# New orders for the first of two attention blocks, 46 instead of 42 projections in pairs, and four new figures in the planner

## Chip, core and metric

The kernel runs on one core of one Trainium2 chip. The metric is the device time in microseconds (us); a time stands for several runs by their median. The core has five engines that each work through their own list of instructions: TensorE (PE in the profile; its weight loads are PEld), VectorE (DVE), ScalarE (ACT), GpSimd (POOL) and SyncE (SP), which here issues all the DMAs. They wait for each other by semaphores only.

## What is computed

Two independent attention layers, A and B, each on 2048 tokens of width 512 with 32 heads of 16. Their outputs stand side by side.

```python
qkv = (x @ wqkv).reshape(B, S, 3, H, Dh).transpose(2, 0, 3, 1, 4)
q, k, v = qkv[0], qkv[1], qkv[2]
scores = einsum("bhqd,bhkd->bhqk", q, k) * (Dh ** -0.5)
# A only: idx = arange(S); d = idx[:, None] - idx[None, :]
# A only: scores = where((d >= 0) & (d < 256), scores, -1e9)
o = einsum("bhqk,bhkd->bhqd", softmax(scores), v)
y = o.transpose(0, 2, 1, 3).reshape(B, S, D) @ wo
out = concatenate([y_A, y_B], axis=-1)
```

## The kernel before

**Blocks and units.** Layer A is the first block, layer B the second. A unit is a block, a group g of four heads (0 to 7) and a chunk c of 512 queries (0 to 3): 32 units for each block. A's window lets one query tile see at most three key tiles, so A has little attention work for each unit; B sees all 16.

**Projections.** Queries and keys are projected for a pair of groups p (0 to 3) and a chunk c, values for a chunk c and a token tile a: 32 + 32 + 32 = 96 projections over both layers, all of them made during the first block. Each is 12 matmuls of 512 columns (four slices of the contraction times three products of split float32 parts). `ORDER_P` names them in their order: `Ak12` is layer A, keys, p = 1, c = 2; `Bv30` is layer B, values, chunk 3, tile 0. A projection runs either alone over all 128 rows (`project_qk`, `project_v`, by `products`, L212), or in a pair over two halves of 64 rows (`half_rows`, L340): 24 steps of two concurrent matmuls into two banks, cut into four parts.

Its result leaves PSUM over ACT. For queries and keys (`end_qk`) it is then split into two parts, by POOL (L305, L306) or, for the first group, by ACT and DVE (L291, L301), stored in device memory (`parts`), and read back by `load_k` and `load_q` in the layout that scores need (`opk`, `oq`). Values go to `vd` and come back into `vt`.

**Attention in block A.** For each unit, `max_item` makes score products and their row maxima (L505 on PE, L510 or L514 and L515 on DVE). `max_finish` turns them into three bf16 parts (L567). `max_rows` transposes these on PE (L582), and ACT (`ntr`) and two small DMAs write them as extra rows of `oq` (L589). `scores` (L615) then gives scores less the maximum, ACT takes the exponential (L622), POOL cuts the window's edge (L632), and `weigh` (L661) multiplies by the values. `unit_end`, `invert` and `normalise` bring sums and outputs through device memory.

**The order.** `ORDER_A` writes out PE's order in the first block, one letter for each item:

- `p` a projection alone (PE's full array), `g` one of the four parts of a pair
- `m` a maximum item for two heads, `e` the same for B's first unit from separate copies
- `s` scores of two heads for one step, `w` the weighing of one step (three steps to a unit)
- `t` the transpose of a unit's maxima

p uses the full array, g, m, e and s use row tiles, w and t column tiles. The loop over `todo_a` takes one letter after the other. The order of everything else follows from the class `Model`, a small clock with costs for each engine: `M.run` adds a duration to an engine, `M.dma` an issue on SP, a transfer and a landing, with eight lanes in flight. Follow-up steps wait in the heap `soon` (`after`), loads in `lists`, and both are put into the program as soon as the modelled PE time has reached the modelled time of their operands. The model places instructions only; on the chip each of them waits for its real operands, and each engine keeps its list's order.

PSUM has seven banks for all of this (`M.banks["u"]`) and one for the weighed sums. An m takes two neighbouring banks, an s two, a p one, and a pair two from its first part to its last.

**Block B** runs by fixed patterns (`ORDER`, `LAST`) that neither string touches; the model's figures are used there too, for the place of transfers.

Of the kernel before, what the change touches and what calls it, by code (L numbers as in the profile page):

```python
# [48 lines left out]
FILL = 16  # L49
WARM = 22  # L50
ORDER_P = (
# [4 lines left out]
    "Bk23 Bq21 Bk31 Bk33 Bq22 Bq30 Bq31 Bq10 Bq33 Bk32 Bq32 Bk30 ").split()  # L56
WAKE = 200
LOAD = 105
LEAD = 1400
# [2 lines left out]


ORDER_A = (
    "pppppppmmppmmpmmggmmpptmgmgmmppmmggmmpmsgmsgmmpmstwsmgmmgswssgmsgmmwtgmsgmmpmsgmsgmmpsmwtmswsmswsmmp"
    "smswsmmwtsswmsgsgsmwsmgmgmgmgswmsgmgmtwmsgmsgmswmgmsgmmpsmmwtsmwmspsmwsmmpssmwmstwmmspsmswsmmpmmwsmm"
    "swtsmspmmwsmpmsstwmsmwmsssmwmmmpmsmpmtsmwsmmswmmswssmpsmtwsmswmsmsmmmwmspsmwssmtmwmmswmgmsgmswsmgmmg"
    "mwtsmsmmmmpsmwsssmmwtmswmsmpsmmsmwsmwmsmtsmmswmsmpmmswtmsmswsmsmwssmpmmmwtpsmswmmgmgsmsgmwtmsgsmwmmm"
    "psmswwssspmmspmmtwpmsgmsgmmwwsgmsgmgmsgsmtwwmsgsmgmgsmgswsmgmswsmgmwsmgmsgmstwmsgmsgmwmmstwwssmpsmsw"
    "smgmsgmmpsmgmgmmwtmswmsmpmsmwsmsmmswtmsmpmswsmswmmswtsmsmwmsmpsmswtmmmpmsmwsmwmgsgmstwmsgmsgsewmmmpm"  # L70
    "mgsgmswsmgesgeswmmgmgetwsegsmgmswemspmmswmswesgesgmstwsmgmmgmpemmpesmwtwemmpmsgsmgsmwsgsmgemwmstwmmm"
    "pmsgmsgeswsegesgmswmsgmsgeswsmgsmgmwmsmpmmmpmmspmmmtwww")
LAND = 700
LAND_V = 0
LGAP = 2500
# [4 lines left out]
class Model:  # L80
# [19 lines left out]
        return self.run("PE", turn + ns, *after)  # L100

    def dma(self, kb, *after):
        t = self.run("SP", 450, *after, self.lanes[0]) + 600
        self.t["DMA"] = max(self.t["DMA"], t) + int(4.0 * kb)

        self.lanes = [*self.lanes[1:], self.t["DMA"] + 1300]
        return self.lanes[-1]

    def bank(self, pool, n=0):
# [33 lines left out]
def attention_kernel(ctx: ExitStack, tc: tile.TileContext, xT, wqk, wv, wo, out):  # L143
# [9 lines left out]
    M = Model()  # L153
# [131 lines left out]
    def end_qk(b, p, s, c, bank, ps):  # L285

        n = f"{b}_{p}_{s}_{c}"
        at_most(project_qk, 1)
        two = sb.tile([128, 2, QC], F32R, name=f"st_{n}", tag="st")
        if (b, p) == (0, 0):  # L290
            op = nc.scalar.activation(two[:, 0], ps, AF.Copy)  # L291
            t1 = mark(op, M.run("ACT", 480, M.t["PE"] + WAKE))
        else:
            raw = row(f"raw_{n}")
            op = nc.scalar.activation(raw, ps, AF.Copy)  # L295
            t1 = mark(op, M.run("ACT", 480, M.t["PE"] + WAKE))
            release(bank, t1)

        def sub():
            if (b, p) == (0, 0):  # L300
                nc.vector.tensor_sub(two[:, 1], ps, two[:, 0].bitcast(F32))  # L301
                t = M.run("DVE", 610, t1)
                release(bank, t)
            else:
                nc.gpsimd.tensor_copy(two[:, 0], raw)  # L305
                nc.gpsimd.tensor_sub(two[:, 1], raw, two[:, 0].bitcast(F32))  # L306
                t = M.run("Pool", 2400, t1)
            after(t, lambda: store(t), (project_qk, b, p, s, c))

        def store(t):  # L310
            if (b, p, s) not in parts:
                parts[b, p, s] = dram.tile([2, 128, S], F32, name=f"parts_{b}_{p}_{s}")
            nc.sync.dma_start(parts[b, p, s][:, :, c * QC:(c + 1) * QC].rearrange("p r t -> r p t"), two.bitcast(F32))
            ready["parts", b, p, s, c] = M.dma(512, t)
            slots_st.pop(0)
            slots_st.append(ready["parts", b, p, s, c])
        after(t1, sub, (project_qk, b, p, s, c))

    since = []

    def mark(op, t):

        since.append((t + M.load, len(since), op))
        return t
# [341 lines left out]
    def row(n, shape=(128, QC)):  # L666
        return sb.tile(list(shape), F32, name=n, tag="row", bufs=5)
# [122 lines left out]
    def after(ns, f, key=None):  # L790
        seq[0] += 1
        heapq.heappush(soon, (ns, seq[0], f, key))
# [6 lines left out]
    def at_most(kind, n):  # L799

        while sum(x[3] is not None and x[3][0] == kind for x in soon) > n:
            heapq.heappop(soon)[2]()
# [16 lines left out]
    def bank(n=0):  # L819
        return M.bank("u", n)  # L820
# [9 lines left out]
    def release(b, t):  # L830
        if b is not None:
            M.release(b, t)
# [26 lines left out]
    def operands(it, n=0):  # L859

        f, b, *a = it
        if f == project_qk:
            keys = [("w", b, a[0], a[1])] + [("x", b, a[2], i) for i in range(4)]
            t = (slots_st + [M.NEVER] * 2)[n] - 2700 + LAND_V
        elif f == project_v:
            keys = [("w", b, "v", i) for i in range(4)] + [("x", b, a[0], i) for i in range(4)]
            t = (slots_v + [M.NEVER] * 2)[n] - 2700 + LAND_V
        else:
            keys = [("w", b, "o", i) for i in range(4)] + [("o", b, i, a[0]) for i in range(4 if len(a[1]) == 1 else 3)]
            t = 0  # L870
        return max(t, *(ready.get(k, M.NEVER) for k in keys))
# [133 lines left out]
    while todo_a or gen[0]:  # L1005
# [13 lines left out]
        t = NEVER  # L1019
        if gen[0]:  # L1020
            t = pe
        elif x == "p":
            t = max(bank(), operands(its_a[nb]))
        elif x == "g" and stage == 0:
            t = max(bank(1), operands(its_a[nb]), operands(its_a[nb + 1], int(its_a[nb][0] == its_a[nb + 1][0])))
        elif x == "g":
            t = min(since)[0] if CHUNK * stage == 12 else pe
        elif x == "t" and nts:
            t = max(ready["nm", *nts[0]] + LOAD, bank())
        elif x == "w" and k < i:  # L1030
            un, (m, pieces), a, z = flat[k]
            t = max(*(ready.get(("v", 0, un[1] // 2, y[0]), NEVER) for y in pieces), ready["p", *un, m] + 100,
                    M.bank("o") if a else 0)
        elif x == "s" and i < k + AHEAD and (max_rows, *flat[i][0]) in made:
            t = max(bank(1), ready["q", *flat[i][0]] + LAND)
        elif x == "e":
            t = max(ready.get(("qe",), NEVER), ready.get(("ke", early[ne][2]), NEVER)) + LAND + 1500
            t = max(t, M.pair(), M.t["DVE"] - 300)
        elif x == "m" and not (mxs[nm][2] and (nts or mxs[nm][0][0] and ne < len(early))):
            un, it, z = mxs[nm]  # L1040
            t = max(*(ready.get(("k", *un[:2], c), NEVER) for c in (range(NQC) if un[0] else range(un[2] + 1))),
                    ready.get(("qd", *un), NEVER)) + LAND
            t = max(t, M.pair())
# [105 lines left out]
    while nq < 4 * len(steps):  # L1149
# [3 lines left out]
        for x in ORDER if nm < len(mx) else LAST:  # L1153
            k = ns // HG
            if x == "s" and k < len(steps):
                if ns % HG == 0:
                    t = k * STEP
# [28 lines left out]
            elif x.isdigit():  # L1186
# [19 lines left out]
                elif int(x) == 4 and nm < len(mx):  # L1206

                    t = k * STEP
# [37 lines left out]
```

## Time and profile before

| | |
|---|---|
| median of 3 runs | 1816.94 us (1816.69, 1816.94, 1822.71) |
| profiled execution | 1815.08 us, span 1813.4 us |
| mean granted TensorE clock | 0.998 |
| busy: PE, DVE, ACT, POOL | 99%, 83%, 77%, 36% of the span |
| block A | 0 to about 529 us |
| block B | about 529 us to the end |

In the tables of stretches each engine has its busy time in us and, in brackets, its instructions; then come the granted clock of TensorE (1.00 is full speed), the mean busy share of the 16 DMA engines and what they moved. In lists by time each row has the start and the length in us, the engine, the line and what was written and read; in square brackets stands how long the engine had been idle, and who ended that. PE's ends are modelled, so starts are the better measure. A row with a line first gives a group: its count, its busy time, the mean ns of one, and the idle time ahead of it.

### The profile page before, as it was taken

How to read it: one execution, taken by the hardware profiler on the slowest of the kernel's cores; microseconds unless marked ns; L12 is line 12 of the kernel's file. 1: busy time of each engine (PE TensorE's matmuls, PEld its weight loads, DVE VectorE, ACT ScalarE, POOL GpSimd, SP SyncE). 2: the span in 40 equal slices, each digit the busy share in tenths (PEclk: the TensorE clock that was granted, in tenths of full speed). 3: DMA queues.
4: the chain of work that ended last, by engine and by line, in shares of the span. 5: the costliest groups of instructions: out<-in, count | busy, mean ns of one | idle time of the engine just before them, and what ended most of it. 6: DMA issues, size and time to landing. Idle time of an engine off the chain costs nothing. (4 is left out here: it accounts for less than half of the span.)

```text
span 1813.4 us, 39043 instructions
## 1 busy us (share of the span) xinstructions
PE 1795.6 (99%) x14982; PEld 912.2 (50%) x14982; DVE 1508.8 (83%) x2243; ACT 1398.4 (77%) x2750; POOL 649.0 (36%) x1334
## 2 busy tenths in 40 slices
PE   9999999999999999999999999999999999999998
PEld 6776566767764455444444444444444444443436
DVE  5556776676779776899999999999999999999901
ACT  4465666655569776799999999999999999999983
POOL 0377778664755431042310024320112422022330
PEclk9999999999999999999999999999999999999999
DMA  7766667544573222311201211130031121010012
GB/s 248 218 189 208 190 195 231 173 154 140 162 213 102 77 85 67 82 29 49 61 20 31 63 42 29 29 78 16 16 76 35 29 64 37 17 54 16 24 37 93
DMA packets 129162, 166.80 MB, mean 92 GB/s; under 512 B 23012, under 2 KB 58852, under 8 KB 128964
## 3 DMA queue, kind: packets, MB, share of 16 engines
q1 hardware_dynamic: 128976, 164.31, 30.8%
q8 instruction: 118, 1.93, 0.4%
q14 instruction: 68, 0.56, 0.1%
HBM read 94.49 MB, written 68.19 MB: 90 GB/s over the span
## 5 line engine op out<-in xcount | busy, mean ns | idle before, releaser
L622 ACT ACTIVATE p<-ps_all 128x512 f32<-128x512 f32 x2432 | 1258.1, 597 | 185.0 <-PE ps_all L615 118.6
L462 DVE TENSOR_REDUCE mt<-ps_all 128x2 f32<-128x1024 f32 x1516 | 1195.0, 870 | 63.5 <-PE ps_all L458 52.0
L615 PE MATMUL ps_all<-oq,opk 51*128 51x512 f32 (+2 forms) x2752 | 775.2, 405 | 3.8 <-ACT p L622 2.6
L458 PE MATMUL ps_all<-opk,oq 48*128 48x512 f32 x2016 | 674.5, 438 | 0.4 <-DVE mt L462 0.2
L646 PE MATMUL ps_all<-p,vt 128*17 128x256 f32 (+1 forms) x6056 | 587.7, 460 | 0.5 <-ACT ou L672 0.5
L615 PEld LDWEIGHTS ps_all<-oq,opk 51*128 51x128 f32 x2752 | 398.9, 185 | 181.8 <-ACT p L622 157.7
L458 PEld LDWEIGHTS ps_all<-opk,oq 48*128 48x128 f32 x2016 | 308.7, 184 | 316.5 <-DVE mt L462 179.2
L632 POOL TENSOR_SCALAR_AFFINE_SELECT p<-p 128x256 f32<-128x256 f32 x480 | 178.5, 407 | 111.6 <-ACT p L622 105.1
L646 PEld LDWEIGHTS ps_all<-p,vt 128*17 128x17 f32 x6056 | 100.7, 95 | 223.3 <-issue 212.7
L532 POOL TENSOR_TENSOR mu<-mt 128x16 f32<-128x16 f32 x31 | 6.8, 220 | 508.5 <-DVE mt L462 508.5
L514 DVE COPY_PREDICATED ps_all<-mone,ps_all 128x256 f32<-128x256 uint16 x224 | 95.3, 425 | 99.0 <-PE ps_all L505 89.8
L515 DVE TENSOR_REDUCE nm<-ps_all 128x2 f32<-128x512 f32 x224 | 155.2, 693 | 7.7
L700 POOL TENSOR_TENSOR rd<-ld,minus 128x32 f32<-128x32 f32 x15 | 81.9, 5458 | 218.6 <-DMA ld<-od 218.6
L340 PE MATMUL ps_all<-x,w 64*128 64x512 f32 x672 | 119.9, 392 | 0.0
L212 PE MATMUL ps_all<-x,w 128*128 128x512 f32 x432 | 109.2, 401 | 1.3 <-DVE x L162 0.7
L505 PE MATMUL ps_all<-opk,oq 48*128 48x384 f32 (+2 forms) x512 | 95.7, 369 | 3.8 <-ACT p L622 1.5
L661 PE MATMUL ps_all<-p,vt 128*17 128x384 f32 (+2 forms) x1408 | 97.5, 392 | 0.3 <-POOL p L632 0.2
L212 PE MATMUL ps_all<-w_o,x_o 128*128 128x512 f32 x384 | 92.7, 396 | 0.6 <-ACT ob L765 0.6
L212 PEld LDWEIGHTS ps_all<-x,w 128*128 128x128 f32 x432 | 78.8, 189 | 24.7 <-issue 3.3
L340 PEld LDWEIGHTS ps_all<-x,w 64*128 64x128 f32 x672 | 86.1, 185 | 7.9 <-ACT raw L295 0.3
L295 ACT ACTIVATE raw<-ps_all 128x512 f32<-128x512 f32 x56 | 32.5, 597 | 73.3 <-PE ps_all L212 56.7
L212 PEld LDWEIGHTS ps_all<-w_o,x_o 128*128 128x128 f32 x384 | 70.6, 188 | 30.3 <-issue 12.8
(77 smaller groups left out, 954.1 us busy)
## 6 DMA issues: line engine op xcount, KB each, us to landing
parts<-st SPq DMA_DIRECT2D x64, 512.0 KB
oq<-parts SPq DMA_DIRECT2D x128, 128.0 KB
opk<-parts SPq DMA_DIRECT2D x128, 128.0 KB
od<-ou SPq DMA_DIRECT2D x64, 256.0 KB
vd<-vst SPq DMA_DIRECT2D x32, 272.0 KB
oq<-parts SPq DMA_DIRECT2D x128, 64.0 KB
opk<-parts SPq DMA_DIRECT2D x128, 64.0 KB
t<-od SPq DMA_DIRECT2D x32, 256.0 KB
```

Of the source, the lines that this page charges most:

```text
L212: nc.tensor.matmul(ps, l(u), r(v), start=start and k == 0, stop=stop and k == n - 1)
L340: op = nc.tensor.matmul(view(banks[a ^ turn]), l(u)[rows], r(v)[rows], start=turn == q == 0, stop=turn == 1 and q == 11)
L458: nc.tensor.matmul(ps[:, n], q[rows, 128 * qt:128 * qt + 128], k[rows, kc * QC:kc * QC + QC], start=True, stop=True)
L462: op = nc.vector.tensor_reduce(out=m[:, a:a + len(heads), r, qt, kc], in_=ps, axis=AX.X, op=ALU.max)
L505: nc.tensor.matmul(two[:, a, 0:w], opq[b, g, c][rows, r, 128 * qt:128 * qt + 128], opk2(g)[rows, r, t0:t1], start=True, stop=True)
L514: nc.vector.copy_predicated(two[:, :, 256:384], later, two[:, :, 0:128])
L515: op = nc.vector.tensor_reduce(out=m[:, :, r, qt, 0], in_=two[:, :, 128:384], axis=AX.X, op=ALU.max)
L615: nc.tensor.matmul(ps[x][:, col:col + n1], opk2(g)[rows, pr, 128 * k:128 * k + 128], opq[b, g, c][rows, pr, q0:q0 + n1], start=True, stop= ...
L622: op = nc.scalar.activation(p[:, a0 + x, :w], ps[x][:, :w], AF.Exp, scale=SCALE)
L632: nc.gpsimd.affine_select(out=v, in_=v, pattern=[[0, 2], [sign, 128]], compare_op=ALU.is_ge, fill=zero_fill, base=base, channel_multiplier ...
L646: nc.tensor.matmul(o[32 * j:32 * j + VW, q0:q1], vt[(g // 2) % 2][:, kt, vc:vc + VW], pts[1, g, c, kt, j // 2][:, j % 2, q0:q1], start=kt ...
L661: nc.tensor.matmul(o[32 * j:32 * j + VW, q0:q0 + w], vt[(g // 2) % 2][:, kt, vc:vc + VW], pts[b, g, c, m, j // 2][:, j % 2, col:col + w], ...
```

## The change

`ORDER_P` and `ORDER_A` are replaced: the same projections, maxima, scores, weighings and transposes in another order. The old string has 755 letters with 54 p and 84 g, the new one 759 with 50 p and 92 g. Four figures of the model change: the issue of a DMA (450 ns for all; now 800 for one of 12 KB, 600 for one of 16 KB, 465 for the others), its transfer (4.0 ns per KB; now 3.4), its landing (1300 ns; now 1100) and POOL's split of a projection (2400 ns; now 2000).

```diff
 ORDER_P = (
-    "Aq00 Ak00 Av10 Av00 Aq01 Av13 Ak01 Ak02 Av22 Aq02 Av11 Av01 Av03 Av02 Aq03 Ak03 Av20 Ak12 Av23 Av12 Aq10 "
...
+    "Aq00 Ak00 Ak01 Av10 Av01 Aq01 Av02 Av21 Aq02 Ak02 Av33 Av32 Av00 Ak03 Av03 Aq03 Av11 Av13 Av20 Ak20 Aq11 "
...
 ORDER_A = (
-    "pppppppmmppmmpmmggmmpptmgmgmmppmmggmmpmsgmsgmmpmstwsmgmmgswssgmsgmmwtgmsgmmpmsgmsgmmpsmwtmswsmswsmmp"
-    "smswsmmwtsswmsgsgsmwsmgmgmgmgswmsgmgmtwmsgmsgmswmgmsgmmpsmmwtsmwmspsmwsmmpssmwmstwmmspsmswsmmpmmwsmm"
-    "swtsmspmmwsmpmsstwmsmwmsssmwmmmpmsmpmtsmwsmmswmmswssmpsmtwsmswmsmsmmmwmspsmwssmtmwmmswmgmsgmswsmgmmg"
-    "mwtsmsmmmmpsmwsssmmwtmswmsmpsmmsmwsmwmsmtsmmswmsmpmmswtmsmswsmsmwssmpmmmwtpsmswmmgmgsmsgmwtmsgsmwmmm"
...
-    "pmsgmsgeswsegesgmswmsgmsgeswsmgsmgmwmsmpmmmpmmspmmmtwww")
+    "pppggppppmmggmmpppmgmmgmptmgmmgmpmmgsgmmpsmgmsgmmwtsgsmgmmpsmgsmgmmtwwpsmgsmgmswsmgsmgsmpmmswtwmsspm"
+    "mswwsmgsmgsmwtmgmsgmgsmgmswsmgmsgmswsmgmsgmmtwmgmgmmpsmswtmsmwsswmmpssmwsmmpmstswmmspmswsmswsmmpmmsw"
+    "tmswsmswsmmpmmspmswtmmmpsmswmmmpsmmwtmssmwmssmswmsmpmswsmmswtmsmwmsmssmwsmmpmmstwmswmsgmsgmswsmgmsgm"
+    "mtwmswmssmwmsspmsmwtmsmswmsmmmpmsmwsmmswsmmtswmsmpmmswmtsmwsmssmmwsmpsmwmsmwmmpmsgsmgstwmsgsmgmmwtmm"
...
+    "wmmmpsmgmsgeswsegsmgmswesgmsgeswsmgsmgmwsmmpmsmwwmmmpwtmmmp")
@@ Model.dma
-        t = self.run("SP", 450, *after, self.lanes[0]) + 600
-        self.t["DMA"] = max(self.t["DMA"], t) + int(4.0 * kb)
-        self.lanes = [*self.lanes[1:], self.t["DMA"] + 1300]
+        t = self.run("SP", {12: 800, 16: 600}.get(kb, 465), *after, self.lanes[0]) + 600
+        self.t["DMA"] = max(self.t["DMA"], t) + int(3.4 * kb)
+        self.lanes = [*self.lanes[1:], self.t["DMA"] + 1100]
@@ end_qk, sub
-                t = M.run("Pool", 2400, t1)
+                t = M.run("Pool", 2000, t1)
```

More of the change, by code (lines that the diff above doesn't have):

```diff
@@ L51 @@
 ORDER_P = (
[4 rows of a table removed]
-    "Bk23 Bq21 Bk31 Bk33 Bq22 Bq30 Bq31 Bq10 Bq33 Bk32 Bq32 Bk30 ").split()
[4 rows of a table added]
+    "Bq21 Bq20 Bk33 Bq33 Bq22 Bq32 Bk32 Bk30 Bq11 Bq30 Bk31 Bq31 ").split()
 WAKE = 200
@@ L64 @@
 ORDER_A = (
-    "pppppppmmppmmpmmggmmpptmgmgmmppmmggmmpmsgmsgmmpmstwsmgmmgswssgmsgmmwtgmsgmmpmsgmsgmmpsmwtmswsmswsmmp"
-    "smswsmmwtsswmsgsgsmwsmgmgmgmgswmsgmgmtwmsgmsgmswmgmsgmmpsmmwtsmwmspsmwsmmpssmwmstwmmspsmswsmmpmmwsmm"
-    "swtsmspmmwsmpmsstwmsmwmsssmwmmmpmsmpmtsmwsmmswmmswssmpsmtwsmswmsmsmmmwmspsmwssmtmwmmswmgmsgmswsmgmmg"
-    "mwtsmsmmmmpsmwsssmmwtmswmsmpsmmsmwsmwmsmtsmmswmsmpmmswtmsmswsmsmwssmpmmmwtpsmswmmgmgsmsgmwtmsgsmwmmm"
-    "psmswwssspmmspmmtwpmsgmsgmmwwsgmsgmgmsgsmtwwmsgsmgmgsmgswsmgmswsmgmwsmgmsgmstwmsgmsgmwmmstwwssmpsmsw"
-    "smgmsgmmpsmgmgmmwtmswmsmpmsmwsmsmmswtmsmpmswsmswmmswtsmsmwmsmpsmswtmmmpmsmwsmwmgsgmstwmsgmsgsewmmmpm"
-    "mgsgmswsmgesgeswmmgmgetwsegsmgmswemspmmswmswesgesgmstwsmgmmgmpemmpesmwtwemmpmsgsmgsmwsgsmgemwmstwmmm"
-    "pmsgmsgeswsegesgmswmsgmsgeswsmgsmgmwmsmpmmmpmmspmmmtwww")
+    "pppggppppmmggmmpppmgmmgmptmgmmgmpmmgsgmmpsmgmsgmmwtsgsmgmmpsmgsmgmmtwwpsmgsmgmswsmgsmgsmpmmswtwmsspm"
+    "mswwsmgsmgsmwtmgmsgmgsmgmswsmgmsgmswsmgmsgmmtwmgmgmmpsmswtmsmwsswmmpssmwsmmpmstswmmspmswsmswsmmpmmsw"
+    "tmswsmswsmmpmmspmswtmmmpsmswmmmpsmmwtmssmwmssmswmsmpmswsmmswtmsmwmsmssmwsmmpmmstwmswmsgmsgmswsmgmsgm"
+    "mtwmswmssmwmsspmsmwtmsmswmsmmmpmsmwsmmswsmmtswmsmpmmswmtsmwsmssmmwsmpsmwmsmwmmpmsgsmgstwmsgsmgmmwtmm"
+    "psmswwsmmpmsgmsgmswsgmgmtwsmgmsgmswgmsgmmwwtmsgmsgmswsmgmsgmgmsgmswsmgmsgmmtwwmsgsmgmswtmsgsmgsmwwms"
+    "gmsgmswsmgsmgmtwmmpmmspsmswmmspmsmwsmsmwtmswsmmpmsmwsmsmwtsmswmsmpmsswmmswwmtmmpsmgmsgmswsmgsmgmwtes"
+    "wmmmpmsgmmgstwesgesgmgsmgeswsmgsegeswmmmpmsmwsmwtmgesgmswsmgmsgempemmpmsmwtwemmpmsgsmgswesgsegmmwtms"
+    "wmmmpsmgmsgeswsegsmgmswesgmsgeswsmgsmgmwsmmpmsmwwmmmpwtmmmp")
 LAND = 700
```

6 rows, old and new, of the table ORDER_P are left out of this document.

## The prediction

> **What bounds the kernel now.** I read the page first, then the table of stages, then the list of TensorE's (PE's) instructions in order of time, and last the other engines beside it where PE stands still.
>
> ```profile
> span 1813.4 us, 39043 instructions
> PE 1795.6 (99%) x14982; PEld 912.2 (50%) x14982; DVE 1508.8 (83%) x2243; ACT 1398.4 (77%) x2750; POOL 649.0 (36%) x1334
> core 0: us, PE busy (x) PEld busy (x) DVE busy (x) ACT busy (x) POOL busy (x), PEclk, DMA share, GB/s
> 0.00:529.10 529.10, 517.63 (x4448) 363.22 (x4448) 355.99 (x762) 300.81 (x605) 329.45 (x644) 0.99 0.63 194
> 900.00:1700.00 800.00, 800.00 (x6920) 325.27 (x6922) 800.00 (x1033) 724.57 (x1418) 179.30 (x448) 1.00 0.15 38
> 526.57 2.81 PE L661 MATMUL ps_all<-p,vt 128*17 128x128 f32 x48
> 529.48 0.46 PE L615 MATMUL ps_all<-oq,opk 51*128 51x512 f32 x1
> ```
>
> The last product of block A starts inside the row at 526.57, and block B's first score follows at 529.48. So the change's subject, the order of block A, owns 529.1 of 1813.4 us. Block B, whose text is not changed, has VectorE (DVE) busy 800.00 of 800.00 us in its middle: there a different arrival time moves everything by the same amount, and I carry A's difference to the end one for one. In A, PE is busy 517.63 of 529.10 us; DVE, ScalarE (ACT) and GpSimd (POOL) have a third or more to spare. PE's work bounds A, with 11.47 us in which it stands. Where they are:
>
> ```profile
> 100.00:154.00 54.00, 53.88 (x510) 38.50 (x502) 33.84 (x74) 32.81 (x68) 41.46 (x80) 1.00 0.62 197
> 154.00:202.60 48.60, 47.28 (x408) 29.58 (x407) 34.78 (x81) 31.32 (x65) 35.57 (x70) 1.00 0.73 215
> 202.60:284.30 81.70, 77.55 (x658) 48.65 (x658) 57.66 (x144) 53.14 (x108) 68.69 (x132) 0.96 0.61 185
> 284.30:394.40 110.10, 109.76 (x1055) 78.59 (x1056) 70.61 (x168) 67.94 (x139) 77.96 (x152) 1.00 0.59 189
> 394.40:529.10 134.70, 133.27 (x1216) 95.82 (x1212) 100.79 (x166) 71.94 (x144) 81.22 (x161) 1.00 0.54 170
> ```
>
> PE misses 0.12, 1.32, 4.15, 0.34 and 1.43 us in these five: the loss sits between 154 and 284 us (5.47 us), and there alone the clock falls below 1.00. Finer windows show both dips:
>
> ```profile
> 210.30:213.70 3.40, 2.15 (x16) 1.45 (x15) 2.93 (x9) 3.27 (x8) 3.40 (x8) 1.00 0.60 187
> 213.70:217.20 3.50, 3.50 (x25) 1.70 (x26) 3.29 (x10) 0.48 (x2) 2.62 (x5) 0.56 0.80 221
> 258.30:261.70 3.40, 2.28 (x22) 1.38 (x20) 2.90 (x6) 2.17 (x5) 3.40 (x8) 1.00 0.29 87
> 261.70:265.10 3.40, 3.40 (x28) 1.65 (x26) 2.55 (x8) 2.42 (x6) 3.40 (x8) 0.53 0.42 161
> ```
>
> Twice a stretch in which PE worked 2.15 or 2.28 of 3.40 us is followed by one at about half the clock: 0.44 of 3.50 and 0.47 of 3.40 us, so 1.5 and 1.6 us of PE's work, 3.1 together. Before the first dip stands a run of maxima and scores (letters m and s) without a projection or a weighing between:
>
> ```profile
> 211.85 0.44 PE L615 MATMUL ps_all<-oq,opk 51*128 51x384 f32 x2 [0.54 <-ACT p L622]
> 212.19 0.66 PE L505 MATMUL ps_all<-opk,oq 48*128 48x384 f32 x3
> 213.55 0.44 PE L505 MATMUL ps_all<-opk,oq 48*128 48x384 f32 x2 [0.70 <-ACT p L622]
> ```
>
> PE waits 0.54 and 0.70 us for an exponential that frees a PSUM bank: the short matmuls of such a run come faster than ACT and DVE empty their banks.
>
> **The change part by part.** *The letters.* Old and new order hold the same 280 m, 192 s, 96 w, 33 t, 16 e and 96 projections. 84 g become 92, four to a pair, so 42 projections in pairs become 46, and 54 p become 50.
>
> ```profile
> 24.36 2.88 PE L212 MATMUL ps_all<-w_v,x 128*128 128x512 f32 x12
> 27.08 2.88 PE L212 MATMUL ps_all<-x,w 128*128 128x512 f32 x12
> 36.34 3.01 PE L212 MATMUL ps_all<-x,w 128*128 128x512 f32 x12
> 39.28 0.62 PE L505 MATMUL ps_all<-opk,oq 48*128 48x384 f32 x4
> 39.74 2.90 PE L340 MATMUL ps_all<-w_v,x 64*128 64x512 f32 x24
> 42.48 0.51 PE L505 MATMUL ps_all<-opk,oq 48*128 48x384 f32 x4
> ```
>
> From start to start a projection among projections takes 27.08 - 24.36 = 2.72 us; one between maxima takes 39.28 - 36.34 = 2.94, so one visit of the full array costs 0.22. Half a pair (two g, 24 matmuls) takes 42.48 - 39.74 = 2.74, a pair 5.48, two projections 5.44. A pair saves only visits: four p less and two pairs more is +0.08 us. Counted in the two strings, the full array is entered 44 times before and 42 after (after the first p), and left 45 times before and, with the last p, which leads into block B, 43 after: 2 visits less, 0.44 us. Entries of column-tiled work (w, t) fall from 93 to 91; I price one like half a visit, 0.11, so 0.2 us. Together -0.44 - 0.2 + 0.08 = **-0.6 us**, between 0 (if the turns hide under other waits) and -1.0 (both ends of every visit at full price). The Trainium skill, TensorEngine Tiling (Array Packing), Tiling Modes, says that a change of tiling mode drains the TensorE; the 0.22 us agree. The same page, Restrictions and Gotchas, speaks against the change: row tiling raises PSUM pressure, since row tiles may not share a bank. The trace doesn't bear that out here: 284.30 to 394.40 holds ten of the 21 pairs and PE stands only 0.34 us in it. If two more pairs brought one bank wait each like those of 0.54 and 0.70 us, the sum would be smaller by 1.2 us.
>
> *The start.* The third projection is now Ak01 instead of Av10.
>
> ```profile
> 10.14 4.15 PE L212 MATMUL ps_all<-x,w 128*128 128x512 f32 x17 [0.23 <-DVE x L162]
> 15.49 0.49 PE L212 MATMUL ps_all<-w_v,x 128*128 128x512 f32 x1 [1.21 <-ACT w_v L161]
> 16.30 5.50 PE L212 MATMUL ps_all<-w_v,x 128*128 128x512 f32 x23 [0.31 <-DVE w_v L162]
> 13.16 1.28 DVE L162 TENSOR_TENSOR x<-in,x 128x512 fp32r<-128x512 f32 x2
> 15.56 2.49 DVE L162 TENSOR_TENSOR w_v<-in_v,w_v 128x512 fp32r<-128x512 f32 x4
> ```
>
> Av10 waits 1.21 + 0.31 = 1.52 us for the split of w_v. Ak01 needs the key weights, which the second projection used, and four slices of x, whose last split ends at 13.16 + 1.28 = 14.44, before it is reached; when the Av10, Av01 pair comes some 2.7 us later, at about 17, its first slices of w_v are split, and all at 18.05. **-1.5 us**, which is all the wait there is; the other bound is 0 (another operand of the third projection is as late).
>
> *The middle.* It holds 5.47 us of idle and 3.1 of dips. What feeds them is runs of m, s and t. Between the 48th and the 108th s (old: 180 to 315 us) the old string has 8 runs of five or more such letters, the new one 7; of six or more 3 and 2; of four or more 11 and 14. Projections, as work between the runs: old 4, 2, 3, 3, 3, 6 per twelve s from the 36th on, new 3, 4, 2, 3, 2, 6. That is hardly less crowded. I take one eighth of the idle (0.7) and one third of the dips (1.0): **-1.7 us**; between -8.6 (all gone) and +3.6 (40% more, as the poorest stretches with two are two now instead of one).
>
> *The rest of A.* After the 108th s runs of five or more fall from 2 to 0; PE misses 0.34 + 1.43 us there, and part is a wait for a DMA:
>
> ```profile
> 397.58 0.44 PE L505 MATMUL ps_all<-opk,oq 48*128 48x384 f32 x1 [0.38 <-ACT p L622]
> 428.82 0.41 PE L505 MATMUL ps_all<-opk,oq 48*128 48x384 f32 x1 [0.22 <-DMA oq<-parts]
> 429.98 0.41 PE L505 MATMUL ps_all<-opk,oq 48*128 48x384 f32 x1 [0.76 <-DMA oq<-parts]
> ```
>
> The first kind goes (0.38, and the 0.34 taken for the same), the second I leave: **-0.7 us**; between -1.8 and +1.5. The end has three m and a projection behind the last t where three w stood: 3 x 0.23 (two m took 39.74 - 39.28 = 0.46) + 2.72 = 3.4 us to cover the last rows' transfer instead of 529.48 - 526.57 = 2.9. Zero; if the cover fell away, up to these 3 us of waiting would show.
>
> *The constants* of the planner put no instruction on the chip; they move where SP's transfers and the evictions behind them stand in each engine's list.
>
> ```profile
> L305 POOL CAST st<-raw 128x512 fp32r<-128x512 f32 x55 | 33.6, 611 | 19.2 <-DMA parts<-st 11.0 <-ACT raw L295 8.2
> L306 POOL TENSOR_TENSOR st<-raw,st 128x512 fp32r<-128x512 f32 x55 | 70.6, 1284 | 4.6
> L589 SPq DMA_DIRECT2D oq<-ntr x66: 703/725/1942, 52.6 to 528.0; - x66
> L693 SPq DMA_DIRECT2D ld<-od x15: 632/649/661, 148.2 to 517.9; - x15
> 180.80:202.60 21.80, 21.07 (x181) 12.31 (x179) 17.96 (x37) 14.28 (x31) 14.31 (x27) 1.00 0.79 219
> 230.50:256.50 26.00, 24.96 (x211) 15.55 (x208) 19.98 (x50) 16.40 (x36) 19.73 (x38) 1.00 0.79 226
> 284.30:315.10 30.80, 30.65 (x257) 21.39 (x258) 17.79 (x48) 18.40 (x40) 22.99 (x42) 1.00 0.81 251
> ```
>
> POOL's two instructions take 611 + 1284 = 1895 ns: 2000 is nearer than 2400. Issues of 725 and 649 ns are nearer 800 and 600 than 450. At a share of 0.79 the transfers move 219 GB/s, 277 at full share, 3.7 ns per KB (of 1024): between the old 4.0 and the new 3.4. The plan fits the trace better on the whole, on transfers not clearly. I add nothing, with -1 to +9 us as bounds (the upper end in the last rival).
>
> Sum: -0.6 - 1.5 - 1.7 - 0.7 = -4.5 us. The profiled execution took 1815.08 us around its span of 1813.4, which gives 1810.6; the median of the three runs, 1816.94, lies 1.86 above it, which gives **1812.4 us**.
>
> **The rivals.** *The waits only move* (0.25). DVE, ACT and POOL work in list order, so a run that is broken in one place reappears in the next twelve s. For it: 11 runs of four or more become 14. Only start and visits stay, -2.1 us, and half of that is lost again: 1816.
>
> *The middle comes clean* (0.13). If no stretch of some 3.4 us has a third of it idle, both dips and their waits go: -8.6 instead of -1.7, 1805.5. The rows at 210.30 and 258.30 speak for it, the 7 runs left against it. The Trainium skill, TensorE: Matmul & The Clock Gate, HAM oscillation, gives "no PE-idle gaps >~3.4µs" as the rule, by which no order with waits of under a microsecond has a dip, and the sum would lose its 1.0 for them: 1813.4. The trace disagrees (0.54 and 0.70 us stand before a dip); it fits the section behind, on PSUM-queue cycling, where micro-idles re-throttle.
>
> *Too early* (0.14, the other side). With 3.4 ns per KB and 1.1 us where 4.0 and 1.3 stood, work is listed sooner after its transfer. Engines keep list order: an m that waits for oq, as at 428.82, holds every s and w behind it, and a split on ACT that waits for its load holds the exponentials. The price: the three stretches with a share near 0.8 move 21.8 x 219 + 26.0 x 226 + 30.8 x 251 = 18.4 MB, 18,000 KB; at 0.6 ns each, 10.8 us if PE waited out every one. With only start and visits gained, 1816.94 - 2.1 + 10.8 = 1825.6, and more where the waits bring further dips of 1.5 us. It decides from about 5 us on, half of these landings. Against it: PE waited only 0.98 us at 428 to 430 for such a transfer.
>
> **How the numbers follow.** The forecast has 0.48 and a range of its own from 1807.5 to 1815.5. What is within 0.5%, 9.1 us, is about what a measurement of this kernel can tell from no change: below 1807.9 is faster, above 1826.0 slower. Faster, 0.17: the clean middle (0.12) and the forecast's lower end (0.05). Slower, 0.09: the worse part of the last rival. Same, 0.74. The range of 1804.5 to 1823 leaves out some 0.07 below and 0.12 above.
>
> **What would show it.** Right: the third projection starts without w_v as releaser; block A's last matmul lies near 525 us, B unchanged in length; one dip of the clock between 150 and 290 us; in the stage table the idle there near 4.8 us. Wrong: PE's releasers in A name DMAs for several us (too early); three or more dips; block B longer or shorter by over 2 us.

## The result: 2 us faster, and a new wait in the middle

| | before | changed |
|---|---|---|
| median of 20 runs each | 1816.78 us | 1814.78 us |
| median in the second comparison | 1818.4 us (17 runs) | 1814.09 us (12 runs) |
| profiled execution, its span | 1815.08, 1813.4 us | 1817.04, 1815.3 us |

The ratio is 0.9986 with a 95% interval of 0.9977 to 0.9996, and in the second comparison 0.9975 (0.9961 to 0.9989). So some 2 to 4 us are gained, and the profiled execution of the changed kernel is one of its longer ones. Its page, head and first row:

```profile
span 1815.3 us, 39121 instructions
PE 1792.1 (99%) x15030; PEld 911.2 (50%) x15030; DVE 1508.8 (83%) x2243; ACT 1400.6 (77%) x2750; POOL 648.4 (36%) x1334
```

To compare orders that differ, I cut block A where both have done about the same: at the first s after the 36th (36 projections in both), at the first after the 108th (57 before, 56 after) and at the first score of B. The new middle also holds three m and one t less, some 0.9 us at the prediction's 0.23 us each. The table of stretches, first of the kernel before, then of the changed kernel's two profiled executions (the second is `after_again` below):

```profile
0.00:154.00 154.00, 149.77 (x1120) 110.58 (x1120) 92.15 (x204) 76.49 (x150) 66.00 (x133) 1.00 0.70 216
154.00:315.10 161.10, 155.48 (x1321) 99.61 (x1322) 110.23 (x272) 102.85 (x213) 127.25 (x242) 0.98 0.69 207
315.10:529.50 214.40, 212.67 (x2015) 153.07 (x2011) 154.02 (x286) 121.47 (x243) 136.59 (x271) 1.00 0.53 168
529.50:1813.40 1283.90, 1277.67 (x10534) 548.93 (x10534) 1152.38 (x1482) 1097.57 (x2145) 319.16 (x691) 1.00 0.19 50
```

```profile
0.00:153.20 153.20, 148.53 (x1144) 111.57 (x1146) 92.03 (x204) 76.58 (x151) 65.50 (x132) 1.00 0.72 221
153.20:315.60 162.40, 151.70 (x1312) 98.15 (x1312) 109.22 (x268) 102.66 (x209) 121.59 (x231) 0.96 0.64 196
315.60:529.50 213.90, 213.62 (x2044) 152.62 (x2042) 155.00 (x290) 123.19 (x246) 142.22 (x283) 1.00 0.55 173
529.50:1815.30 1285.80, 1278.28 (x10535) 548.87 (x10534) 1152.55 (x1482) 1098.14 (x2145) 319.09 (x690) 1.00 0.18 50
```

```profile
153.20:309.70 156.50, 148.45 (x1314) 96.26 (x1312) 109.11 (x268) 102.36 (x209) 121.50 (x231) 0.98 0.65 203
309.70:523.40 213.70, 213.42 (x2044) 152.78 (x2042) 154.96 (x290) 123.23 (x246) 142.17 (x283) 1.00 0.54 174
523.40:1810.10 1286.70, 1279.27 (x10535) 548.81 (x10534) 1152.65 (x1482) 1097.93 (x2145) 319.27 (x690) 1.00 0.18 50
```

The first stretch is 0.8 us shorter, the last of A about 0.6 although it holds one projection more, and B is 1.9 or 2.8 us longer. In the middle PE misses 10.7 us (162.40 - 151.70) and 8.05 us, against 5.62 before. Where, the list by time of the changed kernel shows; PE, then POOL, then SP:

```profile
196.93 0.61 PE L661 MATMUL ps_all<-p,vt 128*17 128x256 f32 x4
202.15 1.04 PE L661 MATMUL ps_all<-p,vt 128*17 128x256 f32 x4 [4.60 <-POOL p L632]
...
184.51 0.62 POOL L305 CAST st<-raw 128x512 fp32r<-128x512 f32 x1
...
199.78 0.61 POOL L305 CAST st<-raw 128x512 fp32r<-128x512 f32 x1 [6.05 <-DMA parts<-st]
200.47 1.26 POOL L306 TENSOR_TENSOR st<-raw,st 128x512 fp32r<-128x512 f32 x1
201.69 2.56 POOL L632 TENSOR_SCALAR_AFFINE_SELECT p<-p 128x256 f32<-128x256 f32 x7
...
190.76 0.39 SPq L421 DMA_DIRECT2D vt<-vd  x1
191.24 2.14 SPq L313 DMA_DIRECT2D parts<-st  x1
```

Read from the bottom: SP issues a load of 1088 KB into `vt`, and 0.5 us later the store of a split whose result has two slots (`st`). The store's issue takes 2.14 us instead of a median of 0.38, and its slot is free only at 199.78, 8.5 us after the issue began. GpSimd's next split but one (of projection Ak31) waits for that slot; a row of window selects stands behind it in GpSimd's list (the list shown ends at 204 us, after seven of them), and a weighing on PE waits 4.60 us for the first ones. The clock pays again: the two windows from there on are

```profile
196.00:200.00 4.00, 1.48 (x9) 0.60 (x9) 1.47 (x3) 2.41 (x5) 0.22 (x1) 1.00 1.03 380
200.00:204.00 4.00, 1.85 (x10) 1.02 (x12) 0.12 (x1) 0.60 (x1) 3.91 (x9) 0.53 0.56 151
```

PE works 1.48 of 4 us, the DMA engines are full (share 1.03), and the clock falls to half; the next projection takes 4.17 us instead of 2.9.

### The profile page after: what moved, and what is told of

Same layout as the page of the kernel before. It is cut to its first block, busy times and chain, and to the rows that moved or that the text cites. A ratio compares the mean times of both kernels' runs of the same rounds, so it can differ in the third digit from the quotient of the medians.

```text
span 1815.3 us, 39121 instructions
## 1 busy us (share of the span) xinstructions
PE 1792.1 (99%) x15030; PEld 911.2 (50%) x15030; DVE 1508.8 (83%) x2243; ACT 1400.6 (77%) x2750; POOL 648.4 (36%) x1334
## 5 line engine op out<-in xcount | busy, mean ns | idle before, releaser
L212 PE MATMUL ps_all<-x,w 128*128 128x512 f32 x432 | 112.9, 410 | 1.8 <-ACT x L161 1.2
L340 PE MATMUL ps_all<-x,w 64*128 64x512 f32 x672 | 112.8, 392 | 0.0
L505 PE MATMUL ps_all<-opk,oq 48*128 48x384 f32 (+2 forms) x512 | 90.3, 367 | 2.4 <-DMA oq<-parts 0.6
L340 PEld LDWEIGHTS ps_all<-x,w 64*128 64x128 f32 x672 | 80.1, 185 | 8.2
```

Source lines behind the costliest of these rows:

```text
L212: nc.tensor.matmul(ps, l(u), r(v), start=start and k == 0, stop=stop and k == n - 1)
L340: op = nc.tensor.matmul(view(banks[a ^ turn]), l(u)[rows], r(v)[rows], start=turn == q == 0, stop=turn == 1 and q == 11)
L505: nc.tensor.matmul(two[:, a, 0:w], opq[b, g, c][rows, r, 128 * qt:128 * qt + 128], opk2(g)[rows, r, t0:t1], start=True, stop=True)
```

## The experiments

All ratios are to the kernel before, on the same chip, with their 95% intervals.

**The changed kernel once more.** 

> The changed kernel once more, nothing edited. Theory 1 (a fixed collision): the wait of 4.6 us of a weighing for GpSimd's window selects near 197 us, behind a split whose slot waits for a late store, comes back with 3 us or more, the clock halves behind it, and block A ends near 529 us again. Rival (chance): the wait belongs to that one execution; it is under 1 us here, and block A ends 3 to 7 us earlier, at 522 to 526 us. Time by both: 0.997 to 1.000 of the kernel before.

Ratio 0.9975 (0.9961 to 0.9989). The wait is back (the list of waits in block A: sum in us, number, longest):

```profile
PE ps_all L661 <- POOL p L632: 3.7, 2, 3.3
POOL st L305 <- DMA parts<-st: 18.1, 5, 8.8
```

PE's longest wait is 3.3 us here, again at 197 us, with a dip behind it; GpSimd's in front of it is 4.89 us (the 8.8 is another one, near 303 us, taken up below). But block A ends at 523.4 us instead of 529.5, as the rival had it. The collision is fixed, its size is not, and half of what parts the two profiles is a second dip near 251 us that only the first one has.

**The big load one unit later.** The condition of the loads into `vt`:

```diff
-list_("v", lambda u=u: done["w"] >= u - 2 * NQC and (u < NA or ne == len(early)),
+list_("v", lambda u=u: done["w"] >= u - 2 * NQC + (u < NA) and (u < NA or ne == len(early)),
```

> The changed kernel, with the loads of 1088 KB into vt asked for one unit later in block A (some 12 us), so that the one near 191 us no longer stands ahead of two split stores. Theory 1 (the big load delays the stores, the split on GpSimd waits for its slot, the selects stand behind it): GpSimd's wait of 6 us for the store falls under 3 us, the weighing's wait under 1 us, block A ends at 521 to 525 us, ratio to the kernel before 0.995 to 0.998. Rival 1 (the stores are late by the sum of all traffic, B's x loads above all): the wait stays at 3 us or more, ratio as for the changed kernel, 0.998 to 1.000. Rival 2 (chance): the profile has no such wait, but neither has the changed kernel's second run, and the ratios of the two differ by less than 0.0007.

1806.51 us, ratio 0.9930 (0.9911 to 0.9949): theory 1 by the waits, with a gain above its range, and block A ends at 518.9 us, ahead of the 521 to 525. On the chip the load is issued 9 us later, at 199.80. Without the big load ahead of it the store is issued at 190.14 in 0.38 us, and the split that needs its slot waits 0.88 us. SP, POOL, and the middle of A:

```profile
190.14 0.38 SPq L313 DMA_DIRECT2D parts<-st  x1
...
193.98 0.61 POOL L305 CAST st<-raw 128x512 fp32r<-128x512 f32 x1 [0.88 <-DMA parts<-st]
...
152.30:305.00 152.70, 148.24 (x1312) 96.51 (x1312) 109.54 (x268) 102.68 (x210) 125.08 (x236) 0.98 0.69 208
305.00:518.90 213.90, 213.61 (x2046) 152.82 (x2042) 155.00 (x291) 122.93 (x246) 138.92 (x279) 1.00 0.54 174
518.90:1803.60 1284.70, 1277.77 (x10534) 548.86 (x10534) 1152.29 (x1482) 1097.71 (x2145) 319.11 (x690) 1.00 0.18 50
```

The slot is free 3.8 us after its store's issue instead of 8.5, PE's wait for GpSimd is gone, the middle takes 152.7 us, and PE misses 4.46 us in it.

**Two units later** (`+ 2 * (u < NA)`). 

> The changed kernel with the big loads asked for two units later, some 24 us. Theory (any place off the pair of split stores will do, there is slack until the values are used): as vt_load_later, 0.992 to 0.995. Rival (that run hit a lucky place; each place in the busy stretch has a store behind it): 0.996 to 1.001, with a wait of GpSimd for a store of 4 us or more in another place.

1805.78 us, ratio 0.9929 (0.9906 to 0.9952), with a profile like the last one's. The load now goes out at 208.70 us, so two places off the pair of stores do alike, and the first was not a lucky one. This has the lowest median of all versions run, but cannot be told from one unit later.

**The same edit in the kernel before.** 

> The kernel before with the same edit as vt_load_later. There the load of 1088 KB at 187.8 us is followed by loads of keys and queries, and the next split store is issued only at 198.85 us. Theory (the edit pays only where a split store stands right behind the big load): ratio to the kernel before 0.998 to 1.003. Rival (the big load in this busy stretch costs any order): ratio 0.993 to 0.997, as with the new orders.

Ratio 0.9981 (0.9968 to 0.9994), at the near end of the theory's range. There the load delays only reloads of keys and queries, which have slack; the profile's block A ends at 529.9 us instead of 529.5, so what the 2 to 3 us are is not shown.

**One split later.** Only the list on GpSimd is changed, the load stays:

```diff
-after(t1, sub, (project_qk, b, p, s, c))
+after(max(t1, slots_st[0] + 7000) if (b, p, s, c) == (0, 3, 1, 1) else t1, sub, (project_qk, b, p, s, c))
```

> The changed kernel, with one split on GpSimd, that of projection Ak31 whose slot waits for the late store, listed 7 us of the model's time after the landing it counts on, behind the window selects; the big load stays. Split_listed_later moved that split not at all (its wait of 5.8 us stood in the same place), so it said nothing on this. Theory (list order makes the late store hurt): PE's longest wait for GpSimd falls from 3.3 us or more to under 1 us, the clock has no dip near 200 us, block A ends at 518 to 522 us, ratio 0.992 to 0.996. Rival (the late store itself holds the work: the keys of that projection or the free slot are needed at once): block A ends at 523 us or later, ratio 0.997 or more.

1806.82 us, ratio 0.9934 (0.9913 to 0.9954): the theory's time. Six selects now go ahead of the split, which still waits:

```profile
193.82 1.12 POOL L632 TENSOR_SCALAR_AFFINE_SELECT p<-p 128x256 f32<-128x256 f32 x3 [0.61 <-ACT p L622]
195.54 1.12 POOL L632 TENSOR_SCALAR_AFFINE_SELECT p<-p 128x256 f32<-128x256 f32 x3 [0.59 <-ACT p L622]
199.02 0.61 POOL L305 CAST st<-raw 128x512 fp32r<-128x512 f32 x1 [2.36 <-DMA parts<-st]
```

The store is as late as before (issued at 190.34 us, its slot free at 199.02), but PE has no wait for GpSimd left in block A. The profiled execution is the longest of the six (its span is 1810.0 us), and two of the theory's marks are missing in it: block A ends at 524 us, not 518 to 522, and there is a dip near 200 us, since PE waits 1.1 and 0.4 us at 201 us for reloaded queries. So by the medians the load in front of the store and the list order behind it are both needed for the harm, and taking either away gives about the same time; for the list order no trace shows the clean middle.

**All splits later, a miss.** 

> The changed kernel, with GpSimd's split of a projection listed only once the model has the store before last as landed for 1.5 us; the big load stays where it is. Theory (it is GpSimd's list order that makes the late store hurt: window selects behind the split): the selects near 195 us go first, PE's wait for GpSimd falls from 3.3 to 4.6 us to under 1 us, block A ends at 519 to 523 us, ratio 0.993 to 0.996. Rival (with two slots the late store only shifts the wait to the next projections and scores, or to the reload of keys): block A ends at 523 to 529 us, ratio 0.997 to 1.001.

Ratio 0.9975 (0.9959 to 0.9991), as the changed kernel. The margin of 1.5 us left the split in question where it was, with 5.76 us of waiting, so the run says nothing on list order; its wait of 3.4 us on PE is a third sighting of the collision.

**Orders and figures apart.** 

> The two new orders with the four old figures of the planner: only the orders are changed against the kernel before. Theory (the orders carry the gain, the figures only put work into the lists early): the time is 1811 to 1815 us, ratio 0.997 to 0.9990, and GpSimd waits less for its stores than the 13.0 us of the changed kernel's profile. Rival (order and figures fit only together): the planner holds its PE for the slower transfers, list places fall behind the letters, and the ratio is 1.000 to 1.004 with new waits of PE for transposed rows or for loads.

1828.97 us, ratio 1.0048 (1.0031 to 1.0066), just above the rival's range, and not by its waits. The collision near 200 us is there again: the slot is waited for 7.52 us, PE waits 5.23 us for a select, and 3.83 us at 322 us for a split of value weights. 

> The old orders with the four new figures: only the place of transfers and follow-up steps in the engines' lists changes. Theory (the orders carry the gain): 0.999 to 1.003, with PE's waits for DMAs in block A at 1 to 3 us instead of 1.0. Rival (the figures carry it): 0.997 to 0.999. By the rival of the prediction that work is listed too early: 1.003 to 1.005.

1828.72 us, ratio 1.0050 (1.0033 to 1.0066). Each half alone costs 9 us, so neither half carries the gain. In the second, block A is late by 3 to 4 us, and then B starts late. PE and SP, first of old orders with new figures, then of the kernel before:

```profile
536.59 0.47 PE L615 MATMUL ps_all<-oq,opk 51*128 51x512 f32 x1 [3.37 <-DMA oq<-ntr]
...
533.80 0.34 SPq L707 DMA_DIRECT2D rl<-rd  x1
534.24 1.60 SPq L589 DMA_DIRECT2D oq<-ntr  x2
```

```profile
527.12 1.60 SPq L589 DMA_DIRECT2D oq<-ntr  x2
529.96 0.35 SPq L707 DMA_DIRECT2D rl<-rd  x1
```

By the new figures the store of the reciprocals is listed ahead of the transposed maxima. It waits for DVE (8.1 us in the waits of SP's queue), the urgent rows of `oq` stand behind it on SP, and PE waits 3.37 us, with three dips of the clock in B's first 50 us.

**One figure alone.** 

> The changed kernel with GpSimd's figure back at 2400 ns; orders and the figures of the DMAs stay new. Theory (order and figures fit only together, through the place of each step in the lists): even this one figure, which shifts only stores and reloads by 0.4 us, changes the time by 3 us or more, ratio 1.000 to 1.006. Rival (the loss of new_orders_old_figures comes from the figures of the DMAs alone): 0.996 to 0.999, as the changed kernel.

1826.29 us, ratio 1.0048 (1.0030 to 1.0067). GpSimd's 0.4 us of modelled time are worth 12 us on the chip: PE's waits in block A now have two of over 4 us,

```profile
PE ps_all L661 <- POOL p L632: 4.3, 1, 4.3
PE ps_all L340 <- POOL w_v L162: 4.2, 1, 4.2
```

and there are four dips of the clock. The second wait is for a split of value weights, in front of a pair, and it looks like a second collision of the same kind, behind the next big load into `vt` (issued at 299.62 us here; that this load makes the slot late was not tested). The changed kernel has the late slot too. POOL and PE, first of its second execution, then of this run:

```profile
303.52 0.61 POOL L305 CAST st<-raw 128x512 fp32r<-128x512 f32 x1 [8.82 <-DMA parts<-st]
...
305.44 1.27 POOL L162 TENSOR_TENSOR w_v<-in_v,w_v 128x512 fp32r<-128x512 f32 x1
...
306.77 0.73 PE L340 MATMUL ps_all<-w_v,x 64*128 64x512 f32 x4 [0.96 <-POOL w_v L162]
```

```profile
310.83 0.61 POOL L305 CAST st<-raw 128x512 fp32r<-128x512 f32 x1 [7.80 <-DMA parts<-st]
...
317.56 1.26 POOL L162 TENSOR_TENSOR w_v<-in_v,w_v 128x512 fp32r<-128x512 f32 x1
...
318.87 1.22 PE L340 MATMUL ps_all<-w_v,x 64*128 64x512 f32 x4 [4.19 <-POOL w_v L162]
```

The late slot holds GpSimd 8.82 us in the one and 7.80 in the other. But the split of value weights stands directly behind the late split in the first list, and behind another split and eight selects in the second, so PE pays 0.96 us or 4.19. With all the old figures (`new_orders_old_figures`) the list is the second one, too.

**Seven pairs as single projections.** Between about 275 and 365 us, `ORDER_A` has a p for the first and third g of a pair, and nothing for the second and fourth. 

> The changed kernel with seven of its 23 pairs, those between about 275 and 365 us, as 14 projections alone (first and third part become a whole projection). The working of the prediction: a pair is 5.48 us, two projections between maxima 2 x 2.94 us, so 0.40 us each, 2.8 us longer in that stretch. Rival 1 (a projection alone leaves VectorE and ScalarE without work for 2.9 us, and their backlog then holds PE for banks): 6 us or more, with waits of PE for exponentials or maxima. Rival 2 (pairs save nothing): within 1 us.

Ratio 1.0038 (1.0018 to 1.0058). The stretch from the 96th to the 144th s, of the changed kernel, of its second execution and of this one:

```profile
282.80:397.10 114.30, 111.88 (x1099) 80.13 (x1097) 74.43 (x177) 69.20 (x140) 74.58 (x150) 1.00 0.58 179
```

```profile
278.00:391.10 113.10, 111.62 (x1099) 80.06 (x1097) 74.37 (x177) 69.10 (x140) 74.59 (x149) 1.00 0.57 181
```

```profile
284.80:409.20 124.40, 119.71 (x930) 79.70 (x929) 73.29 (x177) 69.56 (x140) 74.64 (x149) 1.00 0.52 164
```

10.1 to 11.3 us more, 1.4 to 1.6 for a pair: rival 1. PE's waits for exponentials and maxima, which are not among those of the two pair runs in this stretch:

```profile
PE ps_all L615 <- ACT p L622: 3.3, 6, 0.9
PE ps_all L505 <- DVE nm L515: 1.0, 2, 0.5
```

ACT's evictions of queries and keys wait 20.2 us for projections alone to end instead of 6.2 in the second execution. PE's idle time grows only from 1.5 or 2.4 to 4.7 us. Since PE's ends are modelled, the time from each matmul's start to the next one's says more. The projections' own rows take 61.9 us here, and 62.0 and 61.2 with pairs. The rows of maxima and scores take 40.1 us instead of 29.6 and 29.2. Nine steps of over 0.4 us, at the waits, make 7.8 us of them (0.9 and 0.5 before), and the shorter steps grew by 3.6 us, near the 2.8 of the turns.

**B's normalising later.** `vt_load_two_units_later`, with `+ 2000` in `normalise_now` as 9000 for layer A's outputs in B. 

> vt_load_two_units_later, and in block B the normalising of layer A's outputs is listed 7 us later on GpSimd, so that the chain of maxima of B's second unit stands ahead of it. Theory (a normalising of 3.2 us between two parts of that chain makes PE wait 1.2 us at its transposed maxima): PE's wait for nm at L559 goes, the first 64 scores of B take 39.5 us instead of 40.3, and the time is 1 to 2 us under vt_load_two_units_later, ratio 0.991 to 0.994. Rival (the output projections then come late instead): 0.994 to 0.998, with waits of PE at L212 for x_o.

1811.4 us, ratio 0.9960 (0.9944 to 0.9977): slower than without, in the rival's range but without its waits for x_o. The wait stayed at 1.23 us, since another normalising took the place between the parts of the chain. In the profile B has two dips of the clock that the run without the edit has not, from 526 to 532 us and from 706 to 711; by the granted clock they are about 5.0 of the 6.4 us between the two spans. What starts them is not shown.

## Why the prediction came out as it did

*Time and sign* held: forecast 1812.4 us in 1804.5 to 1823, measured 1814.78, and 1814.09 the second time. The size, -4.5 us, stands against -2.0 (interval -0.7 to -4.2) and -4.3. That the sum came near is in part luck: in the first pair of profiles the four stretches of the table differ by -0.8, +1.3, -0.5 and +1.9 us, in the second by -0.8, -4.6, -0.7 and +2.8, where I had -2.1 (the visits put into the first), -1.7, -0.7 and 0. Of my signs, the first projections came as said. The first execution has two dips instead of one, the idle time in the middle is 10.7 and 8.05 us instead of some 4.8, and B's 2.8 us in the second are a sign that I had put under wrong.

*The start* (-1.5) was right, and did not last. The third projection has no wait for w_v any more, and the fourth item starts at 17.21 us instead of 18.92, 1.7 earlier (19.22 in the second execution, which has a dip from 12 to 15 us):

```profile
10.41 6.87 PE L212 MATMUL ps_all<-x,w 128*128 128x512 f32 x29 [0.22 <-DVE x L162]
17.21 3.04 PE L340 MATMUL ps_all<-w_v,x 64*128 64x512 f32 x24
```

At 153 us, with the visits' -0.6 included, 0.8 us are left. One place that takes some back is the first maxima, which now wait 0.25 and 0.21 us for keys at 31.6 us; the rest is small pieces.

*The middle* (-1.7) is the step that failed. I counted what was in the old profile (runs of letters, projections between them) and found it hardly less crowded. That reading fits what the orders are worth without the collision: in `vt_load_later` the middle takes 152.7 us instead of 161.1, which is 5.6 less beside the missing projection of 2.8 us (4.7 beside the m and t as well), well within my bounds. What I left out is what order letters don't show: which transfer stands behind which on SP. In the changed kernel the stretch is 162.4 and 156.5 us, so +4.1 and -1.8 beside the projection, the first of them outside my bounds. Window selects behind one split behind one store behind one load cost 3.3 to 4.6 us of waiting and, with half the clock until about 207 us, 2 to 3 us more.

*The last rival* had the kind of mechanism (a transfer that lands later than its followers in the list assume) but put it on 0.6 ns per KB of every landing, 10.8 us in all. It is single landings: one costs PE 3.3 to 4.6 us in the changed kernel, two cost it over 4 us each in `pool_figure_old`. The old orders with the new figures show a late store on SP at the end of A, with 3.37 us of waiting on PE.

*The clean middle* had 1805.5 us and a chance of 0.13; one edit gave 1806.51, with one dip left near 244 us. PE still misses 4.46 us in the middle there, close to the 4.8 that I gave for the forecast.

*The rest of A* (-0.7) was mis-sized: 0.5 and 0.7 us shorter with one projection more, so about -3.3 and -3.5. The table shows 1.4 us of it as idle time that went (1.73 to 0.28). The stretch holds half a pair more, which explains 0.7 to 0.8 us at the price below; the rest stays open.

*The price of a pair* was mis-sized too: 0.40 us a pair by the turns, 1.4 to 1.6 measured. The turns themselves came out near (3.6 us for seven pairs instead of 2.8). I costed PE's own time, and nothing for the engines behind PE: while a projection alone runs for 2.9 us ACT and DVE run dry, and then PE waits for them. I also misread one stretch: 284.30 to 394.40 holds 288 matmuls of pairs, at 48 a pair six of the 21 pairs and not ten, so its 0.34 us said less than I took from it. The warning of PSUM pressure in the Trainium skill (TensorEngine Tiling (Array Packing), Restrictions and Gotchas) did not show in the seven pairs: with fewer pairs there were more waits, 4.7 us of idle time on PE in the stretch instead of 1.5 or 2.4.

*The constants* (zero) can't be priced alone: without the new orders they cost 9 us, and without them the new orders cost 9 us. The sum of parts that I used assumed independent terms, and these are not. Part of why is shown: the one figure of GpSimd decides how far behind the late split the value weights stand.

*Block B* (unchanged within 2 us) is 1.9 and 2.8 us longer. In the second execution 1.7 us of it are a dip from 531 to 536 us. In both, 1.2 us of it is one wait, PE at the transposed maxima of B's second unit, behind a normalising on GpSimd that stands between two parts of their chain:

```profile
558.22 1.28 POOL L740 TENSOR_TENSOR t<-t,bl 128x512 f32<-128x512 f32 x1
...
565.10 0.23 PE L582 MATMUL ps_all<-ident,nm 128*32 128x128 bf16 x2 [1.21 <-POOL nm L559]
```

In the kernel before, the chain runs through without the normalising, and the wait is not there. That this order causes the wait is argued from the lists only: the one edit meant to undo it did not take the normalising away.

## What to carry to other kernels

An order and the figures of the model that places everything else belong together: here changing either alone cost 9 us, more than the two gained, and a sum of separate terms said little. Before trusting a forecast of a new order, look in each in-order list at what stands behind a transfer that can be late (a store behind the biggest load, an eviction behind a store's slot, short urgent work behind that), since one such chain outweighs dozens of small savings. Moving the big load by 9 us, some 90 us ahead of the first weighing that reads it, took 7.6 us off the changed kernel, about twice what the whole change had gained.

## What was unexpected of the hardware

A store of 512 KB behind a load of 1088 KB on the same queue freed its slot 8.5 us after its issue began, against 3.8 without the load, and its issue alone took 2.14 us instead of 0.38. And a dip of the clock needed no long pause: before the change no wait ahead of the first one was longer than 0.54 and 0.70 us, while in the changed kernel PE stood 0.62 us at 307 us and 1.13 us at 312 us with no dip. In the wait of 4.60 us the clock fell to half and stayed there for about 6.8 us.
